# A chunked delta rule feeding a maxout block: from the second token group on, every engine in the order of the program, with the links laid out by pieces

## The chip, the cores and the metric

The kernel runs on one core of a Trainium2 chip. The metric is the device time of one execution in microseconds. A trace of one execution of the kernel before, taken on the chip, lies beside it; its span is 656.4 us.

## The reference

Two blocks in a row, all in fp32. The attention block is a delta rule over 768 steps for each of 4 batches and 8 heads of size 48; its output, with the heads side by side, is the token matrix x (3072 x 384) of a maxout block:

```python
k_n = k / (norm(k) + 1e-6)
for t in range(S):
    y[t] = q[t] @ state
    v_old = state.T @ k_n[t]
    state = state + beta[t] * outer(k_n[t], v[t] - v_old)
x = y, as (B*S, H*D)
h = maximum(maximum(x @ w1, x @ w2), x @ w3)      # 384 -> 768
out = h @ w_out                                   # 768 -> 384
```

## The kernel before

**Chunks, units and groups.** The 768 steps are cut into 12 chunks of 64. A chunk has two units (n = 2c and 2c + 1), each with two batches in the two halves of the partitions. Two chunks, that is four units and 512 tokens, are a group; there are six. Group m's tokens go through the maxout block, `ffn(m)`, while the recurrence of group m + 1 and the preparation of group m + 2 run beside it.

**The maxout block.** `ffn` is a generator that yields after each *piece*. In a full group there are 22. Pieces 0 to 17 are the hidden ones: for each of six blocks f of 128 hidden columns and each of the three weight matrices, three matmuls of 512 tokens (six instructions in fp32) into a bank of `p_h` (L776). The first matrix's result is copied to h by ScalarE (L784), the other two are folded in with a maximum by VectorE (L786). Pieces 18 to 21 are the output: 128 tokens each, six matmuls over f into `p_o` (L800), a copy by ScalarE (L808) and two stores. `p_h` and `p_o` share two PSUM buffers, so a piece waits for the evacuation of the piece two before it. The first group is cut finer and has 31 pieces.

**The links.** Between pieces the program emits the steps of the recurrence, named by a letter and a number. For a chunk of group m + 1: `k`, `q` (`old_k`, `old_q`: products with the state, then v minus the old value on VectorE, L643, and a copy on ScalarE, L651), `z`, `j` (join the inverses of the two 32-blocks of a chunk), `u` (the new values, L659), `s` (the state, L680 and L686), `y` (L697, L702), `x` (y to DRAM, L732, and read back as `y_q`, L738), `X` (`turn_y`, a block transpose on VectorE into xt, L749). For a unit of group m + 2: `t` (`turn_blocks`: keys and queries, loaded as `turned` by `load_blocks`, are transposed by VectorE, L382) and `g` (`gram`: L402 on TensorE, masked to pt by VectorE, L412, copied to at by ScalarE, L420, and stored to DRAM, L428). The matmul tiles of the links share three PSUM buffers.

**The substitution.** `blocks(m)` reads the diagonal blocks of the Gram matrices back from DRAM into x_bl (L450). `solve(m)` is a generator too: a memset of y_bl, the norms, a scaling (first yield), then 31 steps of forward substitution with two VectorE operations each (L495 and L499), then the write of y_d to DRAM (L503), then for each of two chunks four reads into ut (L512) and the transposes `turn_t1` (L546) that the step j needs. `some(solving, n)` advances it by n yields.

**Norms.** `prep(c)` squares the keys (ScalarE, L267), sums them (VectorE, L268), exchanges halves by DMA (L273), and takes the norm (L245 to L250), by which GpSimd scales v (L277).

**The order.** Each engine runs its instructions in one list, and each waits there for its semaphores. In a stretch under `tc.manual_schedule()` the list is the order in which the program emits; elsewhere a planner orders the instructions at compile time with its own estimates of their durations, and the program's order is only a preference. Before the change the prelude is by hand on all engines, the first group on TensorE alone, and groups 1 to 5 are left to the planner. SyncE's list holds nearly all DMA issues, GpSimd's the loads of queries.

```python
    LINKS = {
        0: "k0 q0", 1: "t0 t1", 2: "g0 g1", 3: "z0 z1", 4: "t2", 5: "j0 j1",
        6: "u0 t3", 7: "g2", 8: "s0", 9: "g3", 10: "k1 q1", 12: "u1 y0", 13: "x0",
        14: "s1", 16: "y1", 17: "x1 X0", 21: "X1",
    }
```

Of the kernel before, what the change touches and what calls it, by code (L numbers as in the profile page):

```python
# [9 lines left out]
FP32 = mybir.dt.float32  # L10
# [11 lines left out]
def kernel(  # L22
# [35 lines left out]
    DM = H * D  # L58
# [129 lines left out]
    def fetch(queue=nc.scalar):  # L188
        if fetched[0] < len(pieces):
            _, src, (a, b) = pieces[fetched[0]]  # L190
            st = work.tile([128, 2 * 384], U32, name="w_bits", bufs=4)
            queue.dma_start(
                out=st.rearrange("p (a b) -> p a b", a=a), in_=src
            )
            staged.append(st)
            fetched[0] += 1
# [63 lines left out]
    def prep_sums(c):  # L260


        ksum, kflip = small("ksum", 2, H), small("kflip", H)
        for g in range(2):
            kk = kpad[(2 * c + g) % NK][:, :, 0:D]
            ksq = work.tile([128, H, D], FP32, name="ksq", bufs=1)
            nc.scalar.square(ksq, kk)  # L267
            nc.vector.tensor_reduce(  # L268
                out=kflip if g else ksum[:, 0], in_=ksq,
                axis=mybir.AxisListType.X, op=ALU.add,  # L270
            )
# [19 lines left out]
    def first_squares():  # L291
        ksum, kflip = small("ksum0", 2, 2, H), small("kflip0", 2, H)
        for n in range(4):
            c, g = divmod(n, 2)
            ksq = work.tile([128, H, D], FP32, name="ksq", bufs=1)
            nc.scalar.square(ksq, kpad[n][:, :, 0:D])
            nc.vector.tensor_reduce(
                out=kflip[:, c] if g else ksum[:, c, 0], in_=ksq,
                axis=mybir.AxisListType.X, op=ALU.add,
            )  # L300
        return ksum, kflip
# [53 lines left out]
    def load_blocks(n):  # L355
        c, g = divmod(n, 2)
        for i in range(2):
            t = turned[n, i] = work.tile(
                [128, 2, TURNED], FP32, name="turned", tag="w_bits", bufs=4
            )  # L360
# [99 lines left out]
    def solve(m):  # L460
# [47 lines left out]
        for cc in range(2):  # L508
            for half in range(2):
                for bb in range(2):  # L510
                    r0 = C * bb + BL * half
                    nc.sync.dma_start(  # L512
                        out=ut[cc][
                            r0 : r0 + BL, :, :, BL * half : BL * (half + 1)
                        ].rearrange("p g h i -> p (g h) i"),
                        in_=y_d[half, cc, 2 * bb : 2 * bb + 2].rearrange(
                            "b h c i -> c (b h) i"
                        ),
                    )
            if m >= FINE:  # L520
                turn_t1(2 * m + cc)
            yield

    def diagonal(t):
# [18 lines left out]
    def turn_t1(c):  # L543

        for bb, g in TILES:
            nc.vector.transpose(  # L546
                out=t1[c % NU][block(bb ^ g), g], in_=ut[c % NU][block(bb), g, :, 0:BL]
            )
# [172 lines left out]
        )  # L721
        copied(c, xt, p_x[:, :, 0 : KT * 128].rearrange("p g (t x) -> p g t x", t=KT))

    yqs = {}

    def y_blocks(c):


        y = yts.pop(c)
        y_d = dram.tile([32, 2, 4, DM], FP32, name="y_x")  # L730
# [5 lines left out]
        y_q = yqs[c] = work.tile([128, 8, 96], FP32, name="y_q", tag="w_bits", bufs=4)  # L736
# [79 lines left out]
    def some(gen, n):  # L816
        for _ in range(n):
            if next(gen, gen) is gen:
                break
# [50 lines left out]
    for n in (6, 7):  # L870
# [30 lines left out]


    LINKS = {
# [3 lines left out]
    }  # L907
    EARLY_LINKS = {
# [9 lines left out]
    BY_CHUNK = dict(  # L918
        z=join_z, j=join_u, k=old_k, q=old_q, u=new, s=step, y=to_y, x=to_x,
        e=halves_z, f=halves_u,  # L920
    )
    BY_UNIT = dict(
        t=turn, g=gram, T=lambda n: turn(n, (1,)), P=lambda n: gram(n, (1,))
    )
    SOLVE = 12

    def links(m, names):
        for name in names.split():
            f, i = name[0], int(name[1])
            if f in "xX" and 2 <= m:  # L930
                if m < GROUPS:
                    (y_blocks if f == "x" else turn_y)(2 * m + i)
            elif f in BY_CHUNK and m < GROUPS:
                BY_CHUNK[f](2 * m + i)
            if f in "TP":
                BY_UNIT[f](i)
                if f == "T" and i + 3 < 11:
                    load_q(i + 3)
            elif f in BY_UNIT and m + 1 < GROUPS:
                n = 4 * (m + 1) + i  # L940
                (turn_blocks if f == "t" and n >= BLOCKS else BY_UNIT[f])(n)


    by_hand = ExitStack()
# [1 line left out]
    for i, _ in enumerate(ffn(0)):  # L946
        some(conv, 1)
        fetch()
        links(0, FIRST.get(i, ""))
# [12 lines left out]
        if i in (15, 18):  # L962
            load_v(4 + i // 18)
        if i in (18, 20):
            prep(4 + i // 20)
        if i == 19:
            blocks(2)
        if i == 21:
            solving = solve(2)
            some(solving, 1)  # L970
        if i >= 21:
            some(solving, 4)
        if i >= 27:
            load_k(i - 15)
            if i < 29:
                load_blocks(i - 15)
    some(solving, 40)
    by_hand.close()

    for m in range(1, GROUPS):  # L980
        for i, _ in enumerate(ffn(m)):
            if m + 3 < GROUPS and 18 <= i < 22:
                n = 4 * (m + 3) + i - 18
                load_k(n)
                if i < 20:
                    load_blocks(n)
            if m + 2 < GROUPS:
                n0 = 4 * (m + 2)
                if i in (1, 3):
                    load_blocks(n0 + 2 + i // 3)  # L990
                if i in (6, 9):
                    load_v(n0 // 2 + (i - 6) // 3)
                if i in (9, 11):
                    prep(n0 // 2 + (i - 9) // 2)
                if i == SOLVE - 2:
                    blocks(m + 2)
                if i == SOLVE:
                    solving = solve(m + 2)
                    some(solving, 1)
                if i >= SOLVE:  # L1000
                    some(solving, 4)
            links(m + 1, LINKS.get(i, ""))
        some(solving, 40)
# [1 line left out]
_INS = ['q', 'k', 'v', 'beta', 'moe_w1', 'moe_w2', 'moe_w3', 'moe_w_out']  # L1005
_OUTS = [((3072, 384), 'float32')]
# [25 lines left out]
```

## Time and profile before

| what | value |
|---|---|
| time, median of 3 (range) | 660.28 us (654.39 to 660.74) |
| span of the traced execution | 656.4 us |
| TensorE busy | 568.7 us, 87% |
| its weight loads | 338.3 us, 52% |
| VectorE busy | 342.9 us, 52% |
| ScalarE, GpSimd busy | 134.6 us, 126.6 us |
| chain that ended last | PE 58%, DVE 22%, DMA 11% |
| p_h, L776, matmul | 315.6 us, 702 of 597 ns |
| h maximum, L786 | 50.2 us, 78 of 644 ns |
| substitution, L495 and L499 | 53.2 us each, 154 of 346 ns |

The first row is the time to be predicted; all others are from one execution. A matmul's mean is its own length, and the matmuls of a run overlap, so the spacing in the timeline is shorter than the mean. The shares are of the whole span, and the stages differ: the first 200 us build up the pipeline and convert the weights, the second to fifth groups run all three activities side by side, the last two have no substitution any more.

### The profile page before, as it was taken

To read this page: it belongs to the slowest core of one execution; us is meant where nothing else is said; L and a number is where in the kernel's file an instruction comes from. 1 tells how busy PE (TensorE), PEld (TensorE's weight loads), DVE (VectorE), ACT (ScalarE), POOL (GpSimd) and SP (SyncE) were. 2 spreads that over 40 slices of the span, in tenths; PEclk is the share of its full clock that TensorE was granted. 3 is DMA by queue.
4 is the path that set the end of the run, shared out by engine and by line. 5 is a ranking of instruction groups with operands and counts; after the bars stand their busy time and mean duration, and the time that the engine had idled before them with its cause. 6 is when DMAs were issued, how large, how long until landed. Compare 5 with 4: busy or idle time off the path is not lost.

```text
span 656.4 us, 18744 instructions
## 1 busy us (share of the span) xinstructions
PE 568.7 (87%) x8126; PEld 338.3 (52%) x8126; DVE 342.9 (52%) x786; ACT 134.6 (21%) x264; POOL 126.6 (19%) x222
## 2 busy tenths in 40 slices
PE   6556977899999999989889976897993699999997
PEld 5446756786556455444445542454552355554444
DVE  3544798785596645983442695353259532211110
ACT  4223454534122122011121110120201020110001
POOL 6222633650320000307000305200000000000000
PEclk9755587999999999999899996898897799999999
DMA  9955965843724353247304355512313300130002
GB/s 158 214 127 112 207 162 136 195 95 78 129 59 96 73 105 67 75 115 180 90 16 73 84 133 132 141 26 43 70 45 82 64 3 1 51 83 13 0 0 49
DMA packets 157139, 58.79 MB, mean 90 GB/s; under 512 B 139136, under 2 KB 151232, under 8 KB 157056
## 3 DMA queue, kind: packets, MB, share of 16 engines
q1 hardware_dynamic: 144608, 42.67, 32.1%
q10 hardware_dynamic: 8576, 8.26, 4.6%
q0 software_dynamic: 3872, 6.66, 4.0%
q8 instruction: 64, 1.05, 0.7%
q14 instruction: 19, 0.16, 0.1%
HBM read 40.21 MB, written 17.30 MB: 88 GB/s over the span
## 4 chain that ended last, share of the span: by engine, by line
PE 58%; DVE 22%; DMA 11%; issue 5%; ACT 2%; POOL 1%; SPq 1%; DVEq 0%; POOLq 0%; ACTq 0%
PE p_h L776 38%; DVE y_bl L499 6%; DVE tmp L495 6%; PE p_o L800 6%; DMA w_bits<-in_moe_w_dram 3%; PE p_g L402 3%; DMA kpad<-in_k_dram 2%; PE p_u L659 2%; DMA y_d<-y_bl 2%; PE p_s L680 1%; PE p_y L697 1%; DMA ut<-y_d 1%; DVE t L546 1%; DVE pt L412 1%; DMA x_bl<-at_d 1%
## 5 line engine op out<-in xcount | busy, mean ns | idle before, releaser
L776 PE MATMUL p_h<-xt,w_sb 128*128 128x512 f32 (+1 forms) x702 | 315.6, 597 | 38.0 <-DVE tmp L495 15.5
L776 PEld LDWEIGHTS p_h<-xt,w_sb 128*128 128x128 f32 x702 | 133.9, 200 | 167.7 <-issue 147.7
L786 DVE TENSOR_TENSOR h<-h,p_h 128x512 f32<-128x512 f32 (+1 forms) x78 | 50.2, 644 | 136.0 <-PE p_h L776 133.3
L800 PE MATMUL p_o<-wo_sb,h 128*128 128x384 f32 x288 | 94.7, 487 | 1.2 <-DVE h L786 1.2
L800 PEld LDWEIGHTS p_o<-wo_sb,h 128*128 128x128 f32 x288 | 54.3, 190 | 40.4 <-DVE h L786 2.7
L277 POOL TENSOR_TENSOR v_t<-v_t,nrm 128x768 f32<-128x768 f32 x12 | 17.8, 1484 | 223.4 <-DVE nrm L250 122.3
L495 DVE TENSOR_TENSOR tmp<-x_bl,y_bl 128x31 f32<-128x31 f32 (+20 forms) x154 | 53.2, 346 | 4.5
L499 DVE TENSOR_TENSOR y_bl<-y_bl,tmp 128x31 f32<-128x31 f32 (+20 forms) x154 | 53.2, 346 | 4.4
L784 ACT COPY h<-p_h 128x512 f32<-128x512 f32 (+1 forms) x39 | 21.6, 553 | 159.3 <-PE p_h L776 159.3
L366 POOL DMA_DIRECT2D turned<-in_q_dram x96 | 52.2, 551 | 2.5 <-issue 2.0
L402 PE MATMUL p_g<-kqt 48*64 48x64 f32 (+1 forms) x1280 | 36.3, 251 | 5.6 <-ACT kqt L342 3.7
L402 PEld LDWEIGHTS p_g<-kqt 48*64 48x64 f32 x1280 | 29.3, 149 | 22.9 <-issue 14.0
L808 ACT COPY o_sb<-p_o 128x384 f32<-128x384 f32 x24 | 11.5, 478 | 89.4 <-PE p_o L800 82.2
L420 ACT COPY at<-p_g 128x512 f32<-128x512 f32 x20 | 11.6, 586 | 87.4 <-DVE pt L412 84.8
L412 DVE TENSOR_TENSOR pt<-p_g,mask 128x512 f32<-128x512 f32 x24 | 16.4, 688 | 22.2 <-PE p_g L402 21.8
L659 PE MATMUL p_u<-v_t,ut 64*64 64x48 f32 x768 | 18.2, 235 | 6.6 <-DVE ut L616 4.5
L238 POOL TENSOR_TENSOR w_sb<-mant,up 128x384 int32<-128x384 int32 x18 | 18.1, 1004 | 28.5 <-DVE mant L234 20.1
L659 PEld LDWEIGHTS p_u<-v_t,ut 64*64 64x64 f32 x768 | 15.8, 149 | 15.0 <-issue 8.6
L382 DVE STREAM_TRANSPOSE kqt<-turned 128x256 f32<-128x256 f32 x48 | 18.5, 422 | 6.1 <-DMA turned<-in_k_dram 3.6
L546 DVE STREAM_TRANSPOSE t<-ut 32x256 f32<-32x256 f32 x48 | 20.8, 433 | 1.7 <-DMA ut<-y_d 1.0
L211 ACT ACTIVATE mant<-w_bits 128x384 f32<-128x384 f32 x24 | 13.3, 555 | 20.5 <-POOL w_sb L238 8.1
L215 POOL TENSOR_SCALAR mant<-mant 128x384 f32<-128x384 f32 x24 | 12.9, 538 | 22.2 <-ACT mant L211 21.0
(99 smaller groups left out, 498.1 us busy)
## 6 DMA issues: line engine op xcount, KB each, us to landing
w_bits<-in_moe_w_dram ACTq DMA_DIRECT2D x14, 384.0 KB
at_d<-at SPq DMA_DIRECT2D x36, 128.0 KB
v_t<-in_v_dram SPq DMA_DIRECT2D x24, 192.0 KB
turned<-in_q_dram POOLq DMA_DIRECT2D x96, 48.0 KB, 2.9
turned<-in_k_dram SPq DMA_DIRECT2D x96, 48.0 KB
out_dram<-o_sb SPq DMA_DIRECT2D x48, 96.0 KB
kpad<-in_k_dram SPq DMA_DIRECT2D x44, 96.0 KB
y_d<-y_bl SPq DMA_DIRECT2D x12, 256.0 KB
```

Source lines behind the costliest of these rows:

```text
L366: (nc.sync, nc.gpsimd)[i].dma_start(out=t[p0 : p0 + 32, bb, at : at + NP * 2 * D].rearrange("p (j x) -> p j x", j=NP), in_=(k, q)[i][2 * b ...
L382: nc.vector.transpose(out=kqts[n][:, :, bb ^ (n % 2), i].rearrange("p j (r tb) -> p j tb r", tb=2), in_=t[:, bb, 32 : 32 + NP * 2 * D].rea ...
L402: nc.tensor.matmul(p_g[rows(bb ^ (g * i)), par, c0 : c0 + C * (1 + whole)], kq[:, 0], kq if whole else kq[:, i],)
L412: nc.vector.tensor_tensor(out=by_par(pt), in0=p_v[:, :, :, 1], in1=mask[:, None, None, :].to_broadcast([128, 2, NP, C]), op=ALU.mult,)
L495: nc.vector.tensor_tensor(out=t_v, in0=row.to_broadcast(t_v.shape), in1=column.to_broadcast(t_v.shape), op=ALU.mult,)
L499: nc.vector.tensor_tensor(out=rest, in0=rest, in1=t_v, op=ALU.subtract)
L546: nc.vector.transpose(out=t1[c % NU][block(bb ^ g), g], in_=ut[c % NU][block(bb), g, :, 0:BL])
L659: nc.tensor.matmul(p_v[rows(bb ^ g), g, h], ut[c % NU][rows(bb), g, h], rhs[rows(bb), g, h],)
L776: nc.tensor.matmul(p_h, w_sb[i][:, t, f * 128 : (f + 1) * 128], xt[:, t, lo : lo + w], start=(t == 0), stop=(t == KT - 1),)
L784: nc.scalar.copy(h, p_h)
L786: nc.vector.tensor_tensor(out=h, in0=h, in1=p_h, op=ALU.max)
L800: nc.tensor.matmul(p_o, hs[f][:, i * 128 : (i + 1) * 128], wo_sb[:, f], start=(f == 0), stop=(f == FT - 1),)
```

## The change

From the second group on all engines take the order of the program. For that the table of links is rewritten so that it holds everything that a group does: the loads of keys (`K`), values (`V`) and blocks (`L`, `N`), the two halves of the norms (`p`, `P`), the read of y_q (`w`) apart from the write of y (`x`), and the transposes of t1 (`d`) apart from the substitution. Gram matrices come as early as pieces 1, 2, 5 and 7; `blocks` stands at piece 9, the substitution starts at piece 11 with three yields to a piece and four from piece 18. Of these the last comes after the piece's links, the others before them. A barrier for the planner (`tc.no_sync_barrier`, no semaphore) separates the first group from the rest. Besides, the staging tag w_bits has five buffers instead of four, and ksq shares the tag "up" with two buffers. Tail loads of the first group move into the table.

```diff
-            st = work.tile([128, 2 * 384], U32, name="w_bits", bufs=4)
+            st = work.tile([128, 2 * 384], U32, name="w_bits", bufs=5)
...
-            ksq = work.tile([128, H, D], FP32, name="ksq", bufs=1)
+            ksq = work.tile([128, H, D], FP32, name="ksq", tag="up", bufs=2)
...
-            if m >= FINE:
-                turn_t1(2 * m + cc)
             yield
...
+    def read_y(c):
+        y_d = yds.pop(c)
+        y_q = yqs[c] = work.tile([128, 8, 96], FP32, name="y_q", tag="w_bits", bufs=5)
...
     LINKS = {
-        0: "k0 q0", 1: "t0 t1", 2: "g0 g1", 3: "z0 z1", 4: "t2", 5: "j0 j1",
-        6: "u0 t3", 7: "g2", 8: "s0", 9: "g3", 10: "k1 q1", 12: "u1 y0", 13: "x0",
-        14: "s1", 16: "y1", 17: "x1 X0", 21: "X1",
+        0: "k0 q0 t0 L2", 1: "g0 t1 L3", 2: "g1 d0 d1", 3: "z0", 4: "z1 t2",
+        5: "j0 g2", 6: "j1 t3", 7: "u0 g3", 9: "s0", 10: "y0", 11: "k1 q1 x0",
+        12: "w0 V0", 13: "u1", 14: "K0 K1 V1", 15: "s1 X0", 16: "K2 K3 p0",
+        17: "y1 x1 p1", 18: "N0 P0", 19: "w1 P1", 20: "X1", 21: "N1",
     }
...
+    RECURS = dict(
         z=join_z, j=join_u, k=old_k, q=old_q, u=new, s=step, y=to_y, x=to_x,
-        e=halves_z, f=halves_u,
+        e=halves_z, f=halves_u, d=turn_t1,
     )
+    MADE = dict(V=load_v, p=prep_sums, P=prep_values)
+    UNIT = dict(t=turn, g=gram, K=load_k, L=load_blocks)
...
+            if f in RECURS and m < GROUPS:
+                RECURS[f](2 * m + i)
+            elif f in MADE and m + 1 < GROUPS:
+                MADE[f](2 * (m + 1) + i)
+            elif f in UNIT and m + 1 < GROUPS:
+                UNIT[f](4 * (m + 1) + i)
+            elif f == "N" and m + 2 < GROUPS:
+                load_blocks(4 * (m + 2) + i)
...
-        if i >= 21:
+        if 21 <= i < 29:
             some(solving, 4)
-        if i >= 27:
-            load_k(i - 15)
-            if i < 29:
-                load_blocks(i - 15)
-    some(solving, 40)
+        if i in (27, 28):
+            load_blocks(i - 15)
     by_hand.close()
 
+
+    tc.no_sync_barrier()
+    by_hand = ExitStack()
+    by_hand.enter_context(tc.manual_schedule())
+    RECURS.update(x=y_blocks, w=read_y, X=turn_y)
+    UNIT.update(t=turn_blocks)
     for m in range(1, GROUPS):
         for i, _ in enumerate(ffn(m)):
-            ...
+            if i < 2:
+                some(solving, 1)
             if m + 2 < GROUPS:
-                ...
+                if i == 9:
                     blocks(m + 2)
-                if i == SOLVE:
+                if i == 11:
                     solving = solve(m + 2)
-                    some(solving, 1)
-                if i >= SOLVE:
-                    some(solving, 4)
+            steps = 4 if i >= 18 else 3
+            if i >= 11:
+                some(solving, steps - 1)
             links(m + 1, LINKS.get(i, ""))
-        some(solving, 40)
+            if i >= 11:
+                some(solving, 1)
+    by_hand.close()
```

More of the change, by code (lines that the diff above doesn't have):

```diff
@@ L294, in first_squares @@
             c, g = divmod(n, 2)
-            ksq = work.tile([128, H, D], FP32, name="ksq", bufs=1)
+            ksq = work.tile([128, H, D], FP32, name="ksq", tag="up", bufs=2)
             nc.scalar.square(ksq, kpad[n][:, :, 0:D])
@@ L358, in load_blocks @@
             t = turned[n, i] = work.tile(
-                [128, 2, TURNED], FP32, name="turned", tag="w_bits", bufs=4
+                [128, 2, TURNED], FP32, name="turned", tag="w_bits", bufs=5
             )
@@ L722, in to_x @@
         copied(c, xt, p_x[:, :, 0 : KT * 128].rearrange("p g (t x) -> p g t x", t=KT))
-    yqs = {}
+    yds, yqs = {}, {}
     def y_blocks(c):
         y = yts.pop(c)
-        y_d = dram.tile([32, 2, 4, DM], FP32, name="y_x")
+        y_d = yds[c] = dram.tile([32, 2, 4, DM], FP32, name="y_x")
         for g in range(2):
@@ L735, in y_blocks @@
             )
-        y_q = yqs[c] = work.tile([128, 8, 96], FP32, name="y_q", tag="w_bits", bufs=4)
+    def read_y(c):
+        y_d = yds.pop(c)
+        y_q = yqs[c] = work.tile([128, 8, 96], FP32, name="y_q", tag="w_bits", bufs=5)
         for a in range(4):
@@ L917 @@
     }
-    BY_CHUNK = dict(
+    RECURS = dict(
         z=join_z, j=join_u, k=old_k, q=old_q, u=new, s=step, y=to_y, x=to_x,
-        e=halves_z, f=halves_u,
+        e=halves_z, f=halves_u, d=turn_t1,
     )
[L922 to L925, printed above, removed]
+    MADE = dict(V=load_v, p=prep_sums, P=prep_values)
+    UNIT = dict(t=turn, g=gram, K=load_k, L=load_blocks)
+    OF_KEYS = dict(T=lambda n: turn(n, (1,)), P=lambda n: gram(n, (1,)))
     def links(m, names):
@@ L929, in links, with queries @@
             f, i = name[0], int(name[1])
[L930 to L941, printed above, removed]
+            if f in RECURS and m < GROUPS:
[6 more added lines that the diff above has]
+                load_blocks(4 * (m + 2) + i)
+    def queries(names):
+        for name in names.split():
+            f, n = name[0], int(name[1])
+            if f not in OF_KEYS:
+                links(0, name)
+                continue
+            OF_KEYS[f](n)
+            if f == "T" and n + 3 < 11:
+                load_q(n + 3)
     by_hand = ExitStack()
@@ L948 @@
         fetch()
-        links(0, FIRST.get(i, ""))
+        queries(FIRST.get(i, ""))
         links(1, EARLY_LINKS.get(i, ""))
@@ L970 @@
             some(solving, 1)
-        if i >= 21:
+        if 21 <= i < 29:
             some(solving, 4)
-        if i >= 27:
-            load_k(i - 15)
-            if i < 29:
-                load_blocks(i - 15)
-    some(solving, 40)
-    by_hand.close()
+        if i in (27, 28):
+            load_blocks(i - 15)
+    by_hand.close()
+    tc.no_sync_barrier()
[3 more added lines that the diff above has]
+    UNIT.update(t=turn_blocks)
     for m in range(1, GROUPS):
         for i, _ in enumerate(ffn(m)):
[L982 to L986, printed above, removed]
-            if m + 2 < GROUPS:
[L988 to L995, printed above, removed]
+            if i < 2:
+                some(solving, 1)
+            if m + 2 < GROUPS:
+                if i == 9:
                     blocks(m + 2)
-                if i == SOLVE:
+                if i == 11:
                     solving = solve(m + 2)
-                    some(solving, 1)
-                if i >= SOLVE:
-                    some(solving, 4)
+            steps = 4 if i >= 18 else 3
+            if i >= 11:
+                some(solving, steps - 1)
             links(m + 1, LINKS.get(i, ""))
-        some(solving, 40)
+            if i >= 11:
+                some(solving, 1)
+    by_hand.close()
 _INS = ['q', 'k', 'v', 'beta', 'moe_w1', 'moe_w2', 'moe_w3', 'moe_w_out']
```

## The prediction

> **What bounds the kernel now.** I read the page's busy table first: TensorE is busy 568.7 of 656.4 us, so at most some 88 us are idle. The cut of the trace into stretches says where. The stretches are the five token groups from the second on, each from its first p_h to the next group's first p_h, found in the TensorE timeline. Columns: length, then busy time of PE, weight load, VectorE, ScalarE, GpSimd, then the granted clock.
>
> ```profile
> 206.75:294.18 87.43, 82.31 (x1246) 44.79 (x1244) 58.28 (x141) 15.19 (x30) 9.21 (x15) 1.00 0.42 90
> 294.18:398.92 104.74, 89.70 (x1372) 48.82 (x1373) 56.20 (x127) 14.83 (x28) 20.07 (x42) 0.93 0.41 92
> 398.92:514.19 115.27, 92.60 (x1244) 48.97 (x1245) 58.30 (x138) 15.10 (x30) 16.76 (x31) 0.87 0.34 76
> 514.19:589.87 75.68, 75.57 (x860) 39.31 (x861) 21.50 (x35) 9.66 (x16) 0.00 (x0) 0.98 0.19 44
> 589.87:656.40 66.53, 61.99 (x157) 29.45 (x155) 8.27 (x12) 5.91 (x11) 0.00 (x0) 0.98 0.07 15
> ```
>
> The first three carry the same work, but take 87, 105 and 115 us, and the clock falls with the length. The TensorE timeline names the holes at the starts of the second to fourth of them:
>
> ```profile
> 294.18 2.81 PE L776 MATMUL p_h<-xt,w_sb 128*128 128x512 f32 x6 [2.71 <-DVE xt L749]
> ...
> 398.92 5.46 PE L776 MATMUL p_h<-xt,w_sb 128*128 128x512 f32 x6 [9.70 <-DVE xt L749]
> ...
> 449.62 6.05 PE L776 MATMUL p_h<-xt,w_sb 128*128 128x512 f32 x10 [1.91 <-ACT h L784]
> ...
> 514.19 12.18 PE L776 MATMUL p_h<-xt,w_sb 128*128 128x512 f32 x24 [15.46 <-DVE tmp L495]
> ```
>
> 27.9 us are idle at three group starts: the next tokens' transpose (xt, L749) stands in VectorE's queue behind substitution steps. Six p_h matmuls (one "piece") take 2.58 us in an unbroken run (46.35 for 108); the 5.46 shows a slow clock after a hole. Four holes of 1.91 us inside groups have another cause: the copy of h stands on ScalarE behind the copy of a Gram matrix.
>
> [...] The trace agrees after 9.70 us (six in 5.46) and 15.46 us (24 in 12.18 instead of 10.3), not after 2.71 (2.81); but it also shows slow matmuls after 1.91 us (ten in 6.05 instead of 4.3). [...] The timelines of the two engines agree: a step of usually 0.25 us took 1.55 beside the scaling of v_t.
>
> ```profile
> 263.24 1.48 POOL L277 TENSOR_TENSOR v_t<-v_t,nrm 128x768 f32<-128x768 f32 x1 [15.13 <-DVE tmp L495]
> 263.27 1.55 DVE L499 TENSOR_TENSOR y_bl<-y_bl,tmp 128x87 f32<-128x87 f32 x1
> ```
>
> **The change, part by part.** Arithmetic is the same. I write out the new order for one full group, from its start.
>
> *TensorE.* Per group: 18 pieces 46.35 us, p_o 15.5 us, links (k and q 4.0, Gram 4.4, z and j 2.7, u, s, y 2.16 each) 17.6 us, and 0.2 us at each of 14 returns from a link to p_h (2.77 for a piece alone, 2.575 in a run): 82.3 us. The first full group confirms the sum: 82.31 busy. Up to the end of piece 11: 12 pieces 30.9, links before it 12.3, 11 returns 2.2, together 45.4 us. Piece 17 and y1 end at 66.7, p_o at 82.2.
>
> *First half (pieces 0 to 10).* Gram matrices come at pieces 1, 2, 5, 7; before, at 2, 2, 7, 9. VectorE has the maxima of two pieces in three (0.60 each in a run), 16 block transposes of 0.43, eight t1 transposes of 0.43, and evacuations; following the queue, each result is ready at least one piece before TensorE needs it. The ScalarE holes go, since a piece's copy of h is emitted before its link's Gram copy. I give the first half no idle time in the first of the three groups.
>
> *Second half.* From piece 11 VectorE is full. Its queue, from its rows and from the spacing in its timeline: memset of y_bl 0.9; norm and scaling of x_bl 3.3 (257.41 to 260.69); 31 substitution steps 23.3 (0.44 for the 31-element pair, 0.92 for the longest, each size twice but one); maxima of pieces 11, 13, 14, 16, 17, 3.0; k1, s1, y1 0.86 each, 2.6; two xt transposes 2.3; four reductions 1.9; two short norms 2.2. Sum 39.5. To this come the two scalings of v_t on GpSimd, now beside substitution steps: 1.3 us lost each from the pair above; two other such pairs lost only 0.7. Total 42.1 us. It starts at 45.5, so the last xt transpose ends at 87.6, and TensorE, done at 82.2, waits **5.3 us**. Within the half TensorE doesn't wait: max 14 ends at 57.3 and is needed at 60.3; max 17 ends at 69.5, needed by the sixth h block of p_o at 69.9. DMA keeps up: x_bl, issued after the last Gram copy, is there by about 43 (in two later groups ScalarE used it 5.6 and 6.2 us after the issue, without a wait); y_q of the second chunk, issued behind out stores on SyncE, lands near 83, before VectorE comes to it at 86.4.
>
> *Group starts.* So the holes of 2.71, 9.70 and 15.46 become three of about 5.3. [...] 2 us more in the next group (measured 1.9 and 2.9). A new wait lies behind the starts of the second and third full group: the k half of the second unit's turned data is issued on SyncE behind y_d and eight ut reads. After the last step: y_d 3.1 to 3.7 until its reads may go, reads 4.3 to 5.4, four issues 1.9, landing 2.2 to 2.9, transposes 1.7. The Gram product at piece 2 can start 12.1 to 14.5 us after the group's start; TensorE arrives at 13.6 with the slow clock. I take 0.1 us and keep 0.9 and more for the range.
>
> *No cost.* The fifth w_bits buffer and ksq in "up": prefetch and norm work of VectorE, ScalarE and GpSimd, behind the first group's matmuls (49.3 of 50 us busy from 150 to 200). I leave that group at 206.75. The moved loads of k, v and blocks are issues on SyncE between pieces 12 and 16, ahead of use; the scheduling barrier adds no semaphore. Both remaining ut reads of the early solve fall in pieces 0 and 1, hidden until z0 at 15.8.
>
> *Sum.* First full group 87.6 (was 87.43); second and third 87.6 + 2 + 0.1 = 89.7 (were 104.74, 115.27); fourth 75.68 + 2.2 for k0, q0 and a return, which before ran ahead of it, = 77.9, its slow start of 1.9 being in already; last 66.5. 206.75 + 87.6 + 89.7 + 89.7 + 77.9 + 66.5 = 618.2 of span, 38.2 less than 656.4. From the median 660.28: **622 us**.
>
> **The rivals.**
> *Forecast, chance 0.58:* VectorE's second half sets the group; 622.
> *TensorE-bound, 0.17:* GpSimd costs VectorE less and the holes shrink to 2.7 with no slow clock: 85.0 three times and 76.0: 604.2 of span, 608 in the median. For it: after 2.71 us the clock stayed up. Against: 39.5 us without any blocking already exceeds TensorE's 36.8.
> *Late transfers, 0.20:* turned data late by 5 us at two starts with 2 us of slow clock each (14), and x_bl landing after 7.3 us, as GpSimd's early issues show, 1.8 late three times (5): 641. [...]
> *A full FIFO jam, 0.05:* each leg of the Gram round trip takes 7.6 us as at the start of the kernel, so substitution starts 7.2 late in three groups (22), each hole costs 2 of clock (6), turned data adds 14 and the shorter y path a few more: 665 to 672, slower than before. Against it: the round trip has ten pieces' time and traffic is about 90 GB/s there, half the start's.
>
> **How the numbers follow.** The time is that of the likeliest. The range reaches over most of both neighbours: 605 (gap-free, and a little) to 642 (late transfers). Faster by over 1%: the first three, 0.93, allowing for jams of middle size; within 1% 0.02; slower 0.05.
>
> **What would show it.** Right: the three full groups between 85 and 92 us; an idle of 4 to 7 us at their ends, released by xt L749; VectorE without idle from piece 11 on; v_t scalings inside substitution; no more 1.91 us holes from h L784. Wrong: idle at p_g of piece 2 released by kqt L382 (late turned data), ScalarE waiting on x_bl, or first full group far from 87.6; the forecast falls altogether if full groups still take over 100 us.

## The result, and the profile after

The changed kernel takes 626.17 us (median of four runs, 623.58 to 627.64) against 659.31 us (654.39 to 660.74) for the kernel before: a ratio of 0.951, with a 95% interval of 0.944 to 0.957. The forecast of 622 us was 4.2 us short. The span of the trace is 623.5 us. Of all executions in this document one, of the new table under the planner, took 820.14 us at a granted clock of 0.64, where the three others of that kernel took 638.39 to 641.22 us at 0.91; it stands in no ratio.

The trace cut into the same stretches as in the prediction: from the first p_h of one group to the first p_h of the next, and the last group. The columns are length, then busy time of PE, weight load, VectorE, ScalarE, GpSimd, then the granted clock. Line numbers of the changed kernel differ by one or two from those of the kernel before: p_h is L777, the maximum of h L787, xt L750.

```profile
209.63:297.47 87.84, 82.21 (x1246) 44.74 (x1244) 60.24 (x138) 16.48 (x31) 21.23 (x41) 0.99 0.51 110
297.47:388.51 91.04, 85.00 (x1245) 45.88 (x1245) 60.35 (x138) 16.04 (x30) 21.84 (x44) 0.97 0.50 110
388.51:477.60 89.09, 85.19 (x1245) 45.88 (x1245) 60.20 (x138) 15.94 (x30) 12.19 (x22) 0.96 0.48 98
477.60:556.86 79.26, 79.14 (x988) 41.15 (x989) 21.54 (x31) 10.51 (x18) 0.00 (x0) 0.96 0.18 44
556.86:623.50 66.64, 62.07 (x156) 29.53 (x156) 8.27 (x12) 5.88 (x11) 0.00 (x0) 1.00 0.06 15
```

The three full groups, which are the second to the fourth (from the fifth on there is no substitution), took 87, 105 and 115 us before and now take 88, 91 and 89. Length minus PE busy is TensorE's idle time: 42.8 us in these three before, 15.6 us now. Their PE busy time fell too, by 12.2 us: the granted clock of the second and third is 0.97 and 0.96 where it was 0.93 and 0.87, and a part of the links (1372 matmuls were counted in one group) is back in its own group. Together that is 39.5 us. Given back are 3.6 us in the group after them (79.26 against 75.68), which now does its own k0 and q0 and loses 2.5 us to a slow start where it lost 1.9 before, and 2.9 us in the first group.

The TensorE timeline of the changed kernel holds three idle stretches from the second group to the fifth, all at group starts. The number in brackets is the idle time before the run and what ended it.

```profile
276.08 15.75 PE L801 MATMUL p_o<-wo_sb,h 128*128 128x384 f32 x48
...
297.47 5.25 PE L777 MATMUL p_h<-xt,w_sb 128*128 128x512 f32 x6 [5.63 <-DVE xt L750]
...
388.51 5.46 PE L777 MATMUL p_h<-xt,w_sb 128*128 128x512 f32 x6 [6.04 <-DVE xt L750]
...
477.60 5.46 PE L777 MATMUL p_h<-xt,w_sb 128*128 128x512 f32 x6 [3.90 <-DVE xt L750]
```

They were 2.71, 9.70 and 15.46. Each is followed by six matmuls in 5.25 to 5.46 us, where an unbroken run takes 2.58; the granted clock is 0.50 in the first 2 us of each. The four holes of 1.91 us behind ScalarE's copy of h are gone.

The last 12 us before the first of these starts, on GpSimd and VectorE:

```profile
286.30 1.47 POOL L277 TENSOR_TENSOR v_t<-v_t,nrm 128x768 f32<-128x768 f32 x1 [49.28 <-DMA ksum<-kflip]
...
286.46 1.53 DVE L499 TENSOR_TENSOR y_bl<-y_bl,tmp 128x192 f32<-128x192 f32 x1
...
294.23 0.21 DVE L499 TENSOR_TENSOR y_bl<-y_bl,tmp 128x31 f32<-128x31 f32 x1
...
296.12 1.20 DVE L750 STREAM_TRANSPOSE xt<-y_q 128x768 f32<-128x768 f32 x1 [1.69 <-DMA y_q<-y_x]
```

Beside the scaling of v_t a substitution step of 0.36 us takes 1.53, as forecast. But the last line was not forecast: VectorE's last step ends at 294.44, and then VectorE itself waits 1.69 us for y_q. So the hole of 5.63 us has two owners: VectorE's list accounts for 3.94 of it, a late transfer for 1.69. Why y_q was late is in SyncE's list, which issues the transfers one after another:

```profile
281.00 1.17 SPq L730 DMA_DIRECT2D y_x<-y  x2
282.27 1.56 SPq L273 DMA_DIRECT2D ksum<-kflip  x2
283.93 1.25 SPq L812 DMA_DIRECT2D out_dram<-o_sb  x2
285.28 4.81 SPq L366 DMA_DIRECT2D turned<-in_k_dram  x8
290.18 1.12 SPq L812 DMA_DIRECT2D out_dram<-o_sb  x2
291.35 2.56 SPq L739 DMA_DIRECT2D y_q<-y_x  x4
```

The eight entries of `turned`, which are one unit's keys, loaded a group early (N0), take 4.81 us of the list, and the read of y_q stands behind them. It lands about 296, some 86.5 us after the group's start.

### The profile page after: what moved, and what is told of

It reads as the page before. It is cut to its first block, busy times and chain, and to the rows that moved or that the text cites. A ratio compares the mean times of both kernels' runs of the same rounds, so it can differ in the third digit from the quotient of the medians.

```text
span 623.5 us, 18714 instructions
## 1 busy us (share of the span) xinstructions
PE 560.9 (90%) x8126; PEld 334.3 (54%) x8126; DVE 348.4 (56%) x786; ACT 137.5 (22%) x264; POOL 126.4 (20%) x222
## 4 chain that ended last, share of the span: by engine, by line
PE 59%; DVE 19%; DMA 12%; SPq 3%; issue 3%; POOL 1%; ACT 1%; ACTq 0%; DVEq 0%; POOLq 0%
PE p_h L777 37%; PE p_o L801 8%; DVE y_bl L499 4%; DVE tmp L495 4%; DMA y_x<-y 3%; PE p_g L402 3%; DMA w_bits<-in_moe_w_dram 3%; PE p_u L657 2%; DVE h L787 2%; PE p_y L695 2%; PE p_j L611 1%; DMA y_d<-y_bl 1%; DMA ut<-y_d 1%; DVE xt L750 1%; PE p_k L629 1%
## 5 line engine op out<-in xcount | busy, mean ns | idle before, releaser
L777 PE MATMUL p_h<-xt,w_sb 128*128 128x512 f32 (+1 forms) x702 | 311.8, 591 | 17.5 <-DVE xt L750 15.6
L777 PEld LDWEIGHTS p_h<-xt,w_sb 128*128 128x128 f32 x702 | 133.0, 199 | 144.2 <-issue 134.3
L787 DVE TENSOR_TENSOR h<-h,p_h 128x512 f32<-128x512 f32 (+1 forms) x78 | 50.2, 644 | 108.1 <-PE p_h L777 107.8
L499 DVE TENSOR_TENSOR y_bl<-y_bl,tmp 128x31 f32<-128x31 f32 (+20 forms) x154 | 59.7, 388 | 5.0
L495 DVE TENSOR_TENSOR tmp<-x_bl,y_bl 128x31 f32<-128x31 f32 (+20 forms) x154 | 50.7, 329 | 4.0
L402 PE MATMUL p_g<-kqt 48*64 48x64 f32 (+1 forms) x1280 | 31.8, 242 | 3.2 <-ACT kqt L342 3.2
L402 PEld LDWEIGHTS p_g<-kqt 48*64 48x64 f32 x1280 | 26.6, 142 | 11.3 <-ACT kqt L342 5.1
L641 DVE TENSOR_TENSOR v_t<-v_t,p_k 128x768 f32<-128x768 f32 x11 | 10.4, 949 | 28.7 <-PE p_k L629 28.7
L657 PEld LDWEIGHTS p_u<-v_t,ut 64*64 64x64 f32 x768 | 14.4, 149 | 14.5 <-issue 8.5
L657 PE MATMUL p_u<-v_t,ut 64*64 64x48 f32 x768 | 16.3, 234 | 5.8 <-DVE ut L614 4.2
L336 PE MATMUL p_t<-ident,qpad 128*128 128x128 f32 x48 | 9.9, 342 | 11.6 <-DMA qpad<-in_q_dram 9.4
L750 DVE STREAM_TRANSPOSE xt<-y_q 128x768 f32<-128x768 f32 x8 | 9.7, 1215 | 17.1 <-DMA y_q<-y_x 17.1
```

The costliest lines, as they stand in the source:

```text
L402: nc.tensor.matmul(p_g[rows(bb ^ (g * i)), par, c0 : c0 + C * (1 + whole)], kq[:, 0], kq if whole else kq[:, i],)
L495: nc.vector.tensor_tensor(out=t_v, in0=row.to_broadcast(t_v.shape), in1=column.to_broadcast(t_v.shape), op=ALU.mult,)
L499: nc.vector.tensor_tensor(out=rest, in0=rest, in1=t_v, op=ALU.subtract)
L657: nc.tensor.matmul(p_v[rows(bb ^ g), g, h], ut[c % NU][rows(bb), g, h], rhs[rows(bb), g, h],)
L777: nc.tensor.matmul(p_h, w_sb[i][:, t, f * 128 : (f + 1) * 128], xt[:, t, lo : lo + w], start=(t == 0), stop=(t == KT - 1),)
L787: nc.vector.tensor_tensor(out=h, in0=h, in1=p_h, op=ALU.max)
```

## The experiments

All ratios are against the kernel before, with 95% intervals. The first three kernels divide the gain among the parts of the change.

**The new table, order left to the planner.** From the changed kernel the strict order is taken away; table, yields, barrier and buffers stay. The kernel was run a second time for a trace.

```diff
     tc.no_sync_barrier()
     by_hand = ExitStack()
-    by_hand.enter_context(tc.manual_schedule())
```

> The new table of links and the barrier, but groups 1 to 5 ordered by the planner again. Theory (the strict order carries the gain, because it keeps the xt transpose out of the middle of the substitution and each h copy ahead of the Gram copy): holes of 8 us or more at xt come back at least at two group starts, 640 to 660 us. Rival (the new places in the table carry it): within 1% of the changed kernel, at most 632 us.

> e1 once more for a trace: about 640 us. Theory: under the planner xt again stands between substitution steps, or a Gram copy ahead of h; idle at xt of 8 us or more at two group starts. Rival: the 15 us to the changed kernel are spread over short waits inside the groups, holes at the starts of 6 us or less.

Measured: 640.37 us (638.39 to 641.22), ratio 0.971 (0.968 to 0.975); the second time, in a single run, 638.34. There the four groups from the second on take 92.5, 97.5, 92.8 and 78.1 us. From the TensorE timeline of that run:

```profile
301.52 15.55 PE L777 MATMUL p_h<-xt,w_sb 128*128 128x512 f32 x30 [4.14 <-DVE xt L750]
...
324.05 4.24 PE L777 MATMUL p_h<-xt,w_sb 128*128 128x512 f32 x6 [1.63 <-ACT h L785]
...
392.04 0.65 PE L402 MATMUL p_g<-kqt 48*64 48x128 f32 x2 [1.61 <-DVE kqt L382]
```

The long waits for xt don't come back: at the starts stand 4.14, 3.46 and 4.13 us. What the planner adds are short waits inside the groups, some 10 us in the three full groups, for the copy of h on ScalarE and for transposed keys among others; and TensorE is busy in these groups for 8.7 us more (261.1 instead of 252.4). Some 2 us of that are k0 and q0 of the fourth group, which come a group early here as before the change; the rest are slow matmuls, such as the six in 4.24 us after the 1.63 above. My theory of holes of 8 us and more fell; the rival, short waits spread over the groups, was right. So the table, with the barrier and the buffers, is worth 2.9%, and the strict order on top of it 2% more. The barrier was not tried alone.

**The strict order, the old table.** The kernel before with groups 1 to 5 by hand, the new buffers, and as little moved as the order allows.

```diff
-        6: "u0 t3", 7: "g2", 8: "s0", 9: "g3", 10: "k1 q1", 12: "u1 y0", 13: "x0",
+        6: "u0 t3", 7: "g2", 8: "s0", 9: "g3", 10: "y0 k1 q1", 12: "u1", 13: "x0",
...
+    tc.no_sync_barrier()
+    by_hand = ExitStack()
+    by_hand.enter_context(tc.manual_schedule())
...
-                if i in (1, 3):
+                if i in (2, 4):
```

> The kernel before, groups 1 to 5 in program order by hand with its own table and loop. Three small edits are needed for a strict order: w_bits with five buffers and ksq in the tag up as in the changed kernel, turned loads at pieces 2 and 4 instead of 1 and 3, y0 ahead of k1. Theory (strict order and new places are both needed): the t1 transposes stand in VectorE's list behind the ut reads and ahead of the last xt transpose, so each of three group starts waits for the round trip y_d to ut, about 8 us, and four transposes more: holes of 9 to 14 us with slow clock after each, 640 to 665 us. Rival (a strict order alone carries the gain): at most 632 us.

Measured: 692.6 us, ratio 1.052 (1.048 to 1.056): slower than before, and above the range of both sides. VectorE's timeline at a group's end, then SyncE's:

```profile
298.90 0.21 DVE L499 TENSOR_TENSOR y_bl<-y_bl,tmp 128x31 f32<-128x31 f32 x1
319.54 1.78 DVE L546 STREAM_TRANSPOSE t<-ut 32x256 f32<-32x256 f32 x4 [20.43 <-DMA ut<-y_d]
...
323.56 1.19 DVE L749 STREAM_TRANSPOSE xt<-y_q 128x768 f32<-128x768 f32 x1
```

```profile
309.08 3.64 SPq L366 DMA_DIRECT2D turned<-in_k_dram  x8
312.82 1.14 SPq L503 DMA_DIRECT2D y_d<-y_bl  x2
317.26 4.29 SPq L512 DMA_DIRECT2D ut<-y_d  x8
```

The substitution is done at 299.1, but the write of its result is issued at 312.8, behind loads; the t1 transposes wait 20.4 us for the data to come back, and xt, which the next group needs, stands behind them on VectorE. TensorE's holes are 21.69, 21.60 and 9.53 us. This is a jam of the kind to which I had given 0.05 in the changed kernel, though through another transfer than the Gram matrices. In the changed table t1 stands apart from the substitution (`d` at piece 2), so that xt has no such wait ahead of it.

**The buffers back.** w_bits has four buffers and ksq one of its own, as before.

```diff
-            st = work.tile([128, 2 * 384], U32, name="w_bits", bufs=5)
+            st = work.tile([128, 2 * 384], U32, name="w_bits", bufs=4)
...
-            ksq = work.tile([128, H, D], FP32, name="ksq", tag="up", bufs=2)
+            ksq = work.tile([128, H, D], FP32, name="ksq", bufs=1)
```

> The changed kernel with w_bits at four buffers and ksq in its own single buffer as before. Theory (the buffers cost and bring nothing): 626 us within 1%, the second group's first p_h still near 209.6 us. Rival 1 (the first group's 2.9 us more come from ksq sharing the tag up): about 623 us, first p_h back near 206.8. Rival 2 (the fifth buffer brings loads early and so part of the gain): 632 us or more, idle at p_g behind turned data.

Measured: 625.4 us, ratio 0.949 (0.945 to 0.954), with the first p_h of the second group at 209.30. The buffers are worth nothing that can be measured in the time, and they did not cause the later start of that group. Within the trace they do something: the holes are 6.44, 6.54 and 5.26 us, 2.7 us longer in sum, and ahead of the third VectorE waits twice 0.59 us for squares, for which the single buffer of ksq is the likely cause. But TensorE is busy for 2.6 us less in these four groups (329.0 instead of 331.5); the six matmuls behind its three holes took 4.37, 5.26 and 4.65 us.

The next three ask who ends the holes at the starts.

**y_q ahead of the keys.** N0 goes one piece later, behind the read of y_q.

```diff
-        17: "y1 x1 p1", 18: "N0 P0", 19: "w1 P1", 20: "X1", 21: "N1",
+        17: "y1 x1 p1", 18: "P0", 19: "w1 N0 P1", 20: "X1", 21: "N1",
```

> The changed kernel with one link moved: N0 (loads of keys for the group after next) from piece 18 to piece 19 behind w1, so that the reads of y_q stand ahead of four key loads in SyncE's list. Theory (the first two holes end on y_q, VectorE alone would give the 3.9 us of the third): all three holes near 3.9 us, 3.5 to 4 us less than the changed kernel, about 622. Rival (VectorE sets the hole, y_q only arrives with it): holes of 5.6, 6.0 and 3.9 stay, 626.

Measured: 626.99 us, ratio 0.951 (0.947 to 0.955). y_q is now in time and xt follows the last step at once; the first two holes fall to 4.75 and 4.73 (a substitution step beside the second scaling of v_t took 2.33 us here instead of 0.25), the third stays at 3.90. But the keys land later. In the next group TensorE waits:

```profile
311.75 1.48 PE L402 MATMUL p_g<-kqt 48*64 48x64 f32 x62 [1.75 <-DVE kqt L382]
```

The gain of 0.9 and 1.3 us at these starts is given back as 1.75, 0.18 and 0.38 us at the Gram products, so the time is the rival's, though the holes are not. This is the wait that the prediction named as the first sign of late turned data; in the changed kernel VectorE waited 0.78 us for these keys, and TensorE not at all.

**No late scaling.** The values of chunks 6 to 11 are not scaled by their norms, so GpSimd's two operations beside the substitution are left out.

```diff
-        scale(c, nrm)
+        if c < 6:
+            scale(c, nrm)
```

> The changed kernel without the scaling of v_t by GpSimd for chunks 6 to 11 (so these chunks use v unscaled). It measures what the two scalings beside the substitution cost. Theory (each blocks one substitution step for about 1.2 us, and VectorE alone sets the third hole while y_q sets the first two): the two long steps of 1.53 us fall to 0.3 to 0.4, the third hole shrinks from 3.9 to about 1.5 us and its slow clock goes; the first two stay at 5.5 to 6; 620 to 623 us. Rival (the scaling costs nothing that counts): 626.

Measured: 620.79 us, ratio 0.944 (0.939 to 0.950). The two steps are back at 0.36 and 0.28 us, so the two scalings had cost VectorE 2.4 us a group. The first two holes hardly move, 5.50 and 5.75; the third falls from 3.90 to 1.89. VectorE's timeline at the first start tells why:

```profile
295.92 1.20 DVE L751 STREAM_TRANSPOSE xt<-y_q 128x768 f32<-128x768 f32 x1 [3.98 <-DMA y_q<-y_x]
```

VectorE (whose xt is L751 in this kernel) is done earlier and waits 2.3 us longer for y_q. So the transfer ends the first two holes, and VectorE's list the third, where N0 is absent (there is no later group to load for); with the shorter list y_q is last there too, by 0.37 us. Against my theory the slow clock after this hole stays:

```profile
474.20 4.51 PE L778 MATMUL p_h<-xt,w_sb 128*128 128x512 f32 x6 [1.89 <-DVE xt L751]
```

**The early keys earlier still.** N0 and N1 are loaded at pieces 13 and 14, ahead of y_q by far.

```diff
-        12: "w0 V0", 13: "u1", 14: "K0 K1 V1", 15: "s1 X0", 16: "K2 K3 p0",
-        17: "y1 x1 p1", 18: "N0 P0", 19: "w1 P1", 20: "X1", 21: "N1",
+        12: "w0 V0", 13: "u1 N0", 14: "K0 K1 V1 N1", 15: "s1 X0", 16: "K2 K3 p0",
+        17: "y1 x1 p1", 18: "P0", 19: "w1 P1", 20: "X1",
```

> The changed kernel with N0 and N1 (all turned loads for the next group's first two units) at pieces 13 and 14 instead of 18 and 21. Theory (SyncE's list: y_q stands behind four key loads, and the second unit's keys behind ut): y_q then lands before VectorE is done, holes of 3.9 to 4.7 at all three starts, no wait at p_g: 3 to 5 us less, 621 to 623. Rival (e4's missing gain had another cause than the turned data): 626 again.

Measured: 625.0 us, ratio 0.952 (0.947 to 0.957). y_q is in time and no Gram product waits, yet the holes are 6.00, 6.00 and 3.89. Now the keys for the norms (K2, K3) stand behind the moved loads, and VectorE's own list, full as it is, waits for their squares in two places:

```profile
280.41 0.55 DVE L268 TENSOR_REDUCE ksum<-ksq 128x8 f32<-128x384 f32 x1 [1.53 <-ACT ksq L267]
...
281.75 0.55 DVE L268 TENSOR_REDUCE kflip<-ksq 128x8 f32<-128x384 f32 x1 [0.79 <-ACT ksq L267]
```

That is 2.3 us, in place of the 1.7 us of y_q. Both moves of one load only passed the delay on to whatever stood behind it.

The last four try to take the holes away. The changes of the second and the third of them are shown against the one before.

**Norms into the first half.** The norms of the next group are computed at pieces 3 to 10, where VectorE has room.

```diff
-        0: "k0 q0 t0 L2", 1: "g0 t1 L3", 2: "g1 d0 d1", 3: "z0", 4: "z1 t2",
-        5: "j0 g2", 6: "j1 t3", 7: "u0 g3", 9: "s0", 10: "y0", 11: "k1 q1 x0",
-        12: "w0 V0", 13: "u1", 14: "K0 K1 V1", 15: "s1 X0", 16: "K2 K3 p0",
-        17: "y1 x1 p1", 18: "N0 P0", 19: "w1 P1", 20: "X1", 21: "N1",
+        0: "k0 q0 t0 L2", 1: "g0 t1 L3", 2: "g1 d0 d1", 3: "z0 V0 K0 K1",
+        4: "z1 t2 p0", 5: "j0 g2 K2 K3", 6: "j1 t3 P0", 7: "u0 g3", 8: "V1 p1",
+        9: "s0", 10: "y0 P1", 11: "k1 q1 x0", 12: "w0", 13: "u1", 15: "s1 X0",
+        17: "y1 x1", 18: "N0", 19: "w1", 20: "X1", 21: "N1",
```

> The changed kernel with the norms' work moved ahead of the substitution: V0 K0 K1 at piece 3, p0 at 4, K2 K3 at 5, P0 at 6, V1 p1 at 8, P1 at 10; N0 and N1 stay. Theory (VectorE's 40 us from piece 11 on set the hole): 6.5 us less in that list (four reductions 1.9, two norms 2.2, two blocked steps 2.4), holes of 1 to 2 us in the first two boundaries and none in the third, and with them no slow clock: 603 to 609 us. Rival (the transfers set it: y_q and the turned data): holes of 4 to 6 us stay and it takes 618 us or more.

Measured: 631.4 us, ratio 0.962 (0.956 to 0.968), slower than the change. The theory fell and the rival was right: VectorE's list now ends early, yet the first two holes are 4.64 and 4.69 us (the third is 1.80), for N0 still stands ahead of the read of y_q, and VectorE waits for it. From VectorE's timeline at the first start (this trace is of the slowest of its runs, 637.0 us):

```profile
302.85 1.20 DVE L750 STREAM_TRANSPOSE xt<-y_q 128x768 f32<-128x768 f32 x1 [6.47 <-DMA y_q<-y_x]
```

What neither side had is a new wait: the keys are loaded only one piece before their squares are wanted. From VectorE's timeline and from TensorE's:

```profile
240.47 0.55 DVE L268 TENSOR_REDUCE ksum<-ksq 128x8 f32<-128x384 f32 x1 [6.43 <-ACT ksq L267]
```

```profile
242.91 4.54 PE L777 MATMUL p_h<-xt,w_sb 128*128 128x512 f32 x6 [3.72 <-DVE h L787]
```

A sum of squares that nobody needs soon blocks VectorE for 6.43 us, the maximum of h stands behind it, and TensorE stops in mid-group for 3.72, 3.47 and 3.06 us, with slow matmuls after the first two (six in 4.54 and 5.46 us).

**The two moves together.** As the last, with N0 at piece 13 and N1 at 14.

```diff
-        9: "s0", 10: "y0 P1", 11: "k1 q1 x0", 12: "w0", 13: "u1", 15: "s1 X0",
-        17: "y1 x1", 18: "N0", 19: "w1", 20: "X1", 21: "N1",
+        9: "s0", 10: "y0 P1", 11: "k1 q1 x0", 12: "w0", 13: "u1 N0", 14: "N1",
+        15: "s1 X0", 17: "y1 x1", 19: "w1", 20: "X1",
```

> e6 and e7 together: norms' work before the substitution, N0 at piece 13 and N1 at 14. Theory: neither VectorE nor SyncE is late any more, holes of at most 1 us, no slow clock at group starts, 600 to 606 us. Rival (TensorE then waits elsewhere, on x_bl or PSUM): 610 or more with new idle inside the groups.

Measured: 620.7 us, ratio 0.942 (0.936 to 0.947), above 610 as the rival had it, though the waits are not at x_bl or PSUM. In its trace (of the fastest of six runs, 613.1 us) the holes at the starts are 1.84, 2.05 and 1.77 us, and six matmuls take 2.81 us after each of them, so that no slow clock shows; idle time for h of 2.78 and 0.90 us remains inside the groups.

```profile
295.46 2.81 PE L777 MATMUL p_h<-xt,w_sb 128*128 128x512 f32 x6 [1.84 <-DVE xt L750]
```

At all three starts VectorE has its list done and waits for y_q, 3.67 to 3.85 us, though no keys stand ahead of the read any more. What is left is the way from y1 to y_q itself, so the next version takes y1 earlier.

**Keys a group ahead.** To the last, the keys for the norms are loaded at pieces 12 and 17 of the group before (a new letter M), and y1, x1 come at pieces 14 and 15. The first group's tail loads its keys again.

```diff
-        0: "k0 q0 t0 L2", 1: "g0 t1 L3", 2: "g1 d0 d1", 3: "z0 V0 K0 K1",
-        4: "z1 t2 p0", 5: "j0 g2 K2 K3", 6: "j1 t3 P0", 7: "u0 g3", 8: "V1 p1",
-        9: "s0", 10: "y0 P1", 11: "k1 q1 x0", 12: "w0", 13: "u1 N0", 14: "N1",
-        15: "s1 X0", 17: "y1 x1", 19: "w1", 20: "X1",
+        0: "k0 q0 t0 L2", 1: "g0 t1 L3", 2: "g1 d0 d1", 3: "z0 V0",
+        4: "z1 t2 p0", 5: "j0 g2", 6: "j1 t3 P0", 7: "u0 g3", 8: "V1 p1", 9: "s0",
+        10: "y0 P1", 11: "k1 q1 x0", 12: "w0 M0 M1", 13: "u1 N0", 14: "y1 N1",
+        15: "s1 X0 x1", 17: "w1 M2 M3", 19: "X1",
...
-            elif f == "N" and m + 2 < GROUPS:
-                load_blocks(4 * (m + 2) + i)
+            elif f in "NM" and m + 2 < GROUPS:
+                (load_blocks if f == "N" else load_k)(4 * (m + 2) + i)
...
+        if i >= 27:
+            load_k(i - 15)
```

> As e8 (norms' work ahead of the substitution, N0 and N1 at pieces 13 and 14), with the two waits seen in e8 taken out: the keys whose squares VectorE waits for are loaded a group ahead (a new letter M at pieces 12 and 17; the first group's tail loads keys 12 to 15 again), and y1 moves from piece 17 to 14, with x1 at 15, w1 at 17, X1 at 19. Theory (e8's idle at h inside the groups comes from the key loads, its 1.8 to 2 us at xt from y_q): no idle over 0.5 us at xt and at h, no slow clock; three full groups near 82.5 us, 594 to 602 us. Rival (TensorE meets a new wait, on x_bl or ut, because VectorE or SyncE is still late): 606 or more.

Measured: 601.4 us (599.7 to 606.5), ratio 0.913 (0.909 to 0.917): as the theory had it. The same stretches of its trace, the last group left out:

```profile
209.66:291.69 82.03, 82.03 (x1246) 44.83 (x1244) 58.07 (x138) 15.66 (x30) 21.57 (x42) 1.00 0.56 120
291.69:373.91 82.22, 82.22 (x1246) 45.04 (x1246) 58.11 (x138) 15.66 (x30) 21.54 (x42) 1.00 0.57 121
373.91:455.94 82.03, 82.03 (x1245) 44.90 (x1244) 57.89 (x138) 15.67 (x30) 12.14 (x21) 1.00 0.45 96
455.94:532.60 76.66, 76.66 (x991) 40.60 (x990) 21.52 (x31) 11.22 (x19) 0.00 (x0) 1.00 0.18 44
```

Length and PE busy are equal to the last digit: TensorE has no hole in these four groups, and its granted clock is 1.00. In them TensorE now sets the time. VectorE works 58 us in each of the three full groups, only 2 us less than in the changed kernel. This version is faster than the kernel before and than the changed one; which part of the gain comes from the keys and which from y1 was not tried apart.

**Only y1 and the loads earlier.** The norms stay beside the substitution, with the scalings; keys and y1 move.

```diff
-        12: "w0 V0", 13: "u1", 14: "K0 K1 V1", 15: "s1 X0", 16: "K2 K3 p0",
-        17: "y1 x1 p1", 18: "N0 P0", 19: "w1 P1", 20: "X1", 21: "N1",
+        12: "w0 V0 K0 K1 K2 K3", 13: "u1 N0", 14: "y1 V1 N1", 15: "s1 X0 x1",
+        16: "p0", 17: "w1 p1", 18: "P0", 19: "X1", 20: "P1",
```

> The changed kernel with the norms' work left beside the substitution, but y1 at piece 14, x1 at 15, w1 at 17 and X1 at 19, keys loaded at 12 ahead of the turned data, N0 and N1 at 13 and 14. VectorE's list from piece 11 on is as long as before (40 us), only the last xt transpose no longer stands at its end. Theory A (the place of xt at the end of the list makes the hole, the length alone does not): no hole over 1 us at the group starts, 598 to 608 us. Theory B (the length of VectorE's second half bounds the group wherever xt stands): the wait moves to p_g, z or j of the next group, groups stay at 86 us or more, 612 to 626 us.

Measured: 609.4 us, ratio 0.924 (0.920 to 0.928), 1.4 us above the range of theory A. xt starts at 293.11 on VectorE with four substitution steps still behind it, and no hole is ended by xt any more. The three full groups take 85.85, 87.45 and 82.15 us, the last of them without a hole, so theory B, by which the length of VectorE's list sets the group, falls. But theory A had no hole over 1 us, and two starts still have one of more than 2. These have a new owner, seen on ScalarE and TensorE:

```profile
294.37 0.48 ACT L809 COPY o_sb<-p_o 128x384 f32<-128x384 f32 x1 [5.89 <-DMA out_dram<-o_sb]
```

```profile
294.90 4.54 PE L777 MATMUL p_h<-xt,w_sb 128*128 128x512 f32 x6 [2.23 <-ACT o_sb L809]
...
382.35 2.84 PE L777 MATMUL p_h<-xt,w_sb 128*128 128x512 f32 x6 [2.25 <-ACT o_sb L809]
```

The copy into o_sb waits 5.89 us for an earlier store of its buffer. That store stands in SyncE's list behind transfers that aren't ready to be issued (the read of y_q alone waits 3.8 us for its write), and p_h waits for the PSUM buffer that the copy frees.

## Why the prediction was right, and where it was off

The mechanism was right in the main: three holes, at the group starts, ended by xt, followed by a slow clock (0.50 in the 2 us after each); none inside the groups. Their sum is 15.6 us, where three of 5.3 make 15.9. That these sums lie so close is in part luck, for VectorE's list, which was to end all three holes, ended only the third; at the first two xt itself waited for y_q. Two of the signs named for being right held only in part: VectorE is idle once after piece 11, in that wait, and the third hole is 3.90 us, just under the 4 to 7. The spans differ by 5.3 us (623.5 against 618.2), which has these terms:

- **First group, 2.9 us.** It was left at 206.75 and took 209.63. The buffers are not the cause (209.30 with them back). In the traces of ten kernels of this study whose first groups differ at most in buffers and in loads at its tail, it ends between 206.9 and 211.9 us. So 206.75, read from the one trace of the kernel before, was probably one draw of a scattered start, and at its low end; the prediction should have given it a few microseconds of range.
- **First full group, 0.2 us.** 82.21 busy and 5.63 idle, forecast 82.3 and 5.3. The TensorE sum is confirmed twice, for the groups of the version with keys a group ahead take 82.03 to 82.22 us without a hole. But within the hole two errors cancel. VectorE's list was shorter than forecast, 40.7 us instead of 42.1 (254.9 to 294.44, and 1.2 for xt), since piece 11 to the last step took less than the rows summed to; the scalings' share of it was right, 2.4 us where 2.6 was forecast. On the other side stood the **arrival of y_q, the step that failed**: forecast 83 us after the start and not limiting, measured some 86.5. The forecast names only out stores ahead of this read in SyncE's list, but N0 stands there too. I had read eight list entries as the loads of two units, and so have four issues of 1.9 us for the keys of one; the eight are one unit's, and take 4.81 us. With N0 behind it the read is issued 3.7 us earlier (287.64 instead of 291.35), which by my estimate brings y_q to about 82.8, as forecast. Without N0 the hole is 3.9 us, as the third one shows.
- **Second full group, 1.3 us.** A hole of 6.04 instead of 5.3, for the same reason, and 2.8 us of slow clock (85.00 busy against 82.21) instead of 2.
- **Third, 0.6 us less.** A hole of 3.90, and 3.0 us of slow clock. That a hole of 5.3 us would slow the clock was my estimate: the trace before showed a granted clock of 0.50 in the 2 us after 9.70 and 15.46 us, and of 1.00 after 2.71, and no hole of a length between at a group start. It held, for after 5.63, 6.04 and 3.90 us the clock is 0.50. But the price of 2 us, taken from 1.9 and 2.9 measured before, was too small.
- **Fourth, 1.4 us.** 76.66 without a hole in the version with keys ahead, where 77.9 less the slow start of 1.9 makes 76.0; the slow start itself cost 2.5.
- **Last, 0.1 us.**

The step from span to median took 1.2 us off: 3.8 us was added for it, 2.7 was right.

The wait for the second unit's turned data came as forecast: VectorE waited 0.78 us for it, TensorE not at all. Of the rivals, the TensorE-bound case fell, for the holes are 3.9 us and more. The late transfers came true in part, at y_q instead of at x_bl or the turned data, for 1.69 and 1.99 us of VectorE's waiting instead of the larger sum. The jam did not come with this table; the old table under the strict order shows one, longer than I had it, and at y_d instead of the Gram matrices.

That "VectorE's second half sets the group" holds for the third group of the changed kernel, but is worded too widely: with the norms taken out of this list, and N0 still ahead of y_q, holes of 4.64 and 4.69 us stayed, and the kernel with y1 earlier has as long a list and no such hole. What counts is the place of xt in that list, at its very end, and when y_q arrives, and not the length alone. That GpSimd's scaling of v_t slows the VectorE step beside it is shown: steps of 1.53 us with the scalings beside them and of 0.36 and 0.28 without.

## What to carry to other kernels

Here a strict program order paid only with a table that gives each link, load and store a place: the same order on the old table cost 5%, the new table under the planner brought 3%, both together 5%. In such lists a moved instruction delays what stands behind it (here VectorE waited 1.69 us for y_q behind the keys, and TensorE 1.75 us at the Gram products with the keys behind y_q), so look, on every engine and on the queue that issues the transfers, at who is next in line, before and after the move. Put what the next stage waits for ahead of long work that nobody waits for, and load its inputs so early, here a group ahead, that no other work in the list is held up by the wait for them.

## What was not expected of the hardware

The length of a hole does not alone decide whether the matmuls behind it are slow. After 1.89 us (the kernel without scaling) and 2.23 us (y1 earlier) six of them took 4.51 and 4.54 us; after 2.25 us in that same run they took 2.84, and after 1.84, 2.05 and 1.77 us (the two moves together) 2.81. In the kernel before, the granted clock in the 2 us after two holes of the same 1.91 us, at 315.07 and 449.62, was 0.76 and 0.50. What else decides was not tried. After the holes of 3.90 to 6.54 us at the group starts of the changed kernel, of the one with the buffers back and of the one with y_q ahead of the keys, six matmuls took 4.20 to 5.46 us, and the slow clock cost 2.5 to 3.0 us each in the changed kernel. But the price is not fixed either. After a third hole of 3.90 us the busy time of the next group lies above the 76.66 us of the version without holes by 2.5 us in the changed kernel, and by 1.35 with y_q ahead of the keys.

Issuing took time too. An entry in SyncE's list took 0.5 to 0.8 us in the stretches shown here (4.81 us for eight, 2.56 for four, 1.17 and 1.56 for two; 3.64 for eight on the old table). And the way through DRAM was long: where the read of y_q was next in line and waited for its write, it was issued 6.8 us after that write (280.86 to 287.64 with y_q ahead of the keys, 280.81 to 287.54 with y1 earlier, where it is 6.7).
